# Inverse stage 1 in blocks of 512 columns, joint evictions of the rest columns, and late F2 in 64-column tiles

## The chip, the cores and the metric

One core of a Trainium2 chip runs the whole program. The metric is the device time of one execution in microseconds; the number given for a kernel is the median of its runs.

## The reference

Two branches work on the same layer-normed input and are joined at the end. `S` is 2048, `D` is 640, `F` is 1728.

```python
xn = _layernorm(q)
# branch A: short shift filter, gate, long convolution by FFT over 2S points, gate
kv = sum(k_pad[:, t:t + S, :] * shift_k[:, ks - 1 - t] for t in range(4)) * v
y  = irfft(rfft(pad(kv)) * rfft(pad(ssm_k)))[:, :S] + kv * ssm_D
s  = xn * y
# branch B: MLP
g  = silu(gelu_tanh(xn @ w1 + b1) @ w2 + b2)
out = q + s * g
```

## The kernel before

The convolution is done as matrix products with tables of sines. The points lie on 128 partitions by 16 tiles of 640 columns. **Stage 1** (`K1`, `K1r` for the filter, `U1`, `U1r` for kv, lines 321 and 332) multiplies each tile by the table `W`; the first 512 columns of a tile are one PSUM tile, and the last 128 columns ("rest") of two tiles share another. They are evicted (`Ke`, `Ker`, `Ue`, `Uer`) into one of four `st` buffers, and each of eight blocks is written to the scratch tensors `scrK` and `scrU` (`Ks`, `Us`) and read back in another layout (`KL`, `UL`). **Stage 2** (`K2`, `U2`, line 500, and `X2` for the rest columns of both, line 515) multiplies by the small table `F2_t` and is evicted in place (`Kf`, `Uf`). Then DVE forms products (`pr`, line 532) into `st` buffers, **inverse stage 1** (`i1`, line 542) multiplies them by the small table `I1_t`, the result is evicted (`ie`) and goes through `scrC` (`cs` writes, `cl` reads); **inverse stage 2** (`i2`, line 568) multiplies by `G`, the transpose of `W`, and DVE multiplies the result into xn (`ym`), adds x (`ad`) and SP stores it (`os`). The kv products are 5 groups on DVE (`kv0` to `kv4`).

The MLP works on four chunks of four tiles. F1 (`f1`, line 402, and `f1h` for the last 64 rows, line 416) gives 14 row blocks of the hidden layer, each followed by a gelu on ACT (`ge`, `geh`); F2 (`f2_i_h`, line 437) does tile i in two column halves of 320, 14 matmuls each, followed by a silu (`si`, line 441) and a product (`gx`, line 443). Transposes of xn (`xt`, line 382) and their evictions (`xe`) come before F1.

PSUM has two small buffers for the MLP (`psf`) and three of two banks for the convolution (`ps`). `evict` (line 166) is a copy on ACT or on DVE, as the order says.

The order of all operations is one list written out by hand, `ORDER`; `Plan.emit` walks through it, takes the first free slot of each pool and emits the operation on its engine (a suffix `/A` or `/D` says ACT or DVE for evictions). Each engine runs its part in that order and waits where an operand or a buffer isn't ready. DMAs are issued from SP's queue, in the same order; a write waits there for its evictions, and what stands behind it waits too.

```python
for n, token in enumerate(tokens):
    ...
    for b in o.bufs:
        ...
        k = next(s for s in slots if all(left[a] == 0 for a in b.pool.after[s]))
    o.fn(e)
```

`warm` (line 594) runs matmuls on zeros at the start. `sm0` (POOL) and `sm1` (DVE) compute the angles for the two small tables, `ss` (ACT, lines 263 and 264) takes their sines.

Of the kernel before, what the change touches and what calls it, by code (L numbers as in the profile page):

```python
# [33 lines left out]
XTD = ()  # L34

# [62 lines left out]
def h3_block(ctx: ExitStack, tc: tile.TileContext, x_d, k_d, v_d, sk_d, K_d, D_d, w1_d, b1_d, w2_d, out_d):  # L98
# [29 lines left out]
    sl_t = [sb.tile([P, H], BF16, name="sl%d" % i)[:] for i in range(3)]  # L128
# [33 lines left out]
    def dmaq(e):  # L162
        return (nc.gpsimd if e == "POOL" else nc.sync).dma_start
# [43 lines left out]
    for g in range(2):  # L207
        a, b = TB[g], TB[g + 1]

        def wq(e, a=a, b=b):  # L210
            n = b - a
            nc.vector.tensor_tensor(out=Pm[:, a:b, :], in0=tq[:, a:b, None].to_broadcast([P, n, 64]),
                                    in1=mq[:, None, :].to_broadcast([P, n, 64]), op=ALU.mult)
            nc.vector.tensor_single_scalar(out=Pc[:, a:b, :], in_=Pm[:, a:b, :], scalar=3 * L // 4, op=ALU.add)
            nc.vector.tensor_single_scalar(out=Pc[:, a:b, :], in_=Pc[:, a:b, :], scalar=L - 1, op=ALU.bitwise_and)
            nc.vector.tensor_single_scalar(out=Pm[:, a:b, :], in_=Pm[:, a:b, :], scalar=L - 1, op=ALU.bitwise_and)
# [18 lines left out]
    def sm1(e):  # L235
# [5 lines left out]
        bit(bi[0], pi, 31, ALU.bitwise_and)  # L241
        bit(bi[1], bi[0], 1, ALU.arith_shift_right)
        bit(bi[2], bi[0], 1, ALU.bitwise_and)
        bit(bi[3], pi, 5, ALU.arith_shift_right)
        bit(bi[3], bi[3], 1, ALU.bitwise_and)
        g.tensor_copy(out=k2s, in_=bi[0])
        g.tensor_copy(out=n2s, in_=bi[1])
        g.tensor_scalar(out=c1s, in0=bi[2], scalar1=16.0, scalar2=None, op0=ALU.mult)
        g.tensor_tensor(out=n2s, in0=n2s, in1=c1s, op=ALU.add)
        g.tensor_scalar(out=c0s, in0=bi[3], scalar1=-8.0, scalar2=24.0, op0=ALU.mult, op1=ALU.add)  # L250
        g.tensor_scalar(out=c1s, in0=bi[3], scalar1=24.0, scalar2=None, op0=ALU.mult)
        for w, c in enumerate((c0s, c1s)):
# [103 lines left out]
    hT, xnT, sl = Pool(hT_t, after=[[], [zb, tmb, smb]]), Pool(xnT_t), Pool(sl_t)  # L356
# [37 lines left out]
    for c in range(NCH):  # L394
        for r, (a, b) in enumerate(((0, 256), (256, 512)) if c == 0 else ((0, 512),)):
            for ft in range(FT - 1):
                pb = Buf(pool=psf)
                nm = "%d_%d_%d" % (c, r, ft)

                def f1(e, c=c, ft=ft, a=a, b=b, pb=pb):  # L400
                    for t in range(DT):
                        nc.tensor.matmul(out=pb.v[:, 0:b - a], lhsT=w1_t[:, ft, t, :], rhs=xnTb[c].v[:, a // P:b // P, t, :],  # L402
                                         start=(t == 0), stop=(t == DT - 1))

                def ge(e, c=c, ft=ft, a=a, b=b, pb=pb):
                    nc.scalar.activation(out=hTb[c].v[:, ft, a:b], in_=pb.v[:, 0:b - a], func=ACT.Gelu_apprx_tanh,  # L406
                                         bias=b1_f[:, ft:ft + 1], scale=1.0)
# [20 lines left out]
    def f2_tile(i):  # L428
        c, q = divmod(i, CH)
        for h in range(2):  # L430
            pb, s_ = Buf(pool=psf), Buf(pool=sl)
            hs = slice(h * H, (h + 1) * H)

            def f2(e, pb=pb, hs=hs):
                for ft in range(FT):
                    M = P if ft < FT - 1 else FLAST + 1
                    nc.tensor.matmul(out=pb.v[:, 0:H], lhsT=hTb[c].v[0:M, ft, q * P:(q + 1) * P], rhs=w2_t[0:M, ft, hs],  # L437
                                     start=(ft == 0), stop=(ft == FT - 1))

            op("f2_%d_%d" % (i, h), "PE", f2, reads=[hTb[c]] + hTf[c] + w2b + oneb, writes=[pb], hold=[s_])  # L440
            op("si_%d_%d" % (i, h), "ACT", lambda e, pb=pb, s_=s_: nc.scalar.activation(  # L441
                out=s_.v, in_=pb.v[:, 0:H], func=ACT.Silu), reads=[pb], writes=[s_])
            op("gx_%d_%d" % (i, h), "DVE", lambda e, s_=s_, hs=hs: nc.vector.tensor_tensor(  # L443
                out=xn_t[:, i, hs], in0=xn_t[:, i, hs], in1=s_.v, op=ALU.mult), reads=[s_], writes=[xnb[i][h]])
# [39 lines left out]
    Kall = []  # L484
    for s in range(NG):
# [33 lines left out]
        for w, (nm, B) in enumerate((("K", Ks), ("U", Us))):  # L519
            op("%sf_%d_2" % (nm, s), "ACT|DVE", lambda e, B=B, pb=pb, w=w: evict(  # L520
                e, B.v[:, :, 512:D].rearrange("p (a r) c -> p a r c", r=2),
                pb.v.rearrange("p a (r w c) -> p a r w c", r=2, w=2)[:, :, :, w, :]), reads=[pb], writes=[sp[nm][2]], hold=[B])
        for hh in range(2):
            hs = slice(hh * H, (hh + 1) * H)
            pr = Buf(pool=st)
            prb = [Buf(), Buf()]
            for w in range(2):
                def prod(e, w=w, hs=hs, Ks=Ks, Us=Us, pr=pr):
                    o = pr.v.rearrange("p a d -> p (a d)").rearrange("p (w a r c) -> p w a r c", w=2, a=2, r=2)[:, w]
                    u = Us.v[:, :, hs].rearrange("p (a r) c -> p a r c", r=2)  # L530
                    k = Ks.v[:, :, hs].rearrange("p (a r) c -> p a r c", r=2)[:, :, w:w + 1, :].to_broadcast([P, 2, 2, H])
                    nc.vector.tensor_tensor(out=o, in0=u, in1=k, op=ALU.mult)  # L532
# [155 lines left out]
```

## Time and profile before

| | |
|---|---|
| median of 3 runs | 193.66 us (193.22 to 194.75) |
| profiled execution | 193.75 us, of which the span is 192.0 us |
| PE busy | 179.7 us, 94% of the span |
| DVE busy | 161.6 us, 84% |
| ACT busy | 139.1 us, 72% |
| DMA | 51.13 MB, 266 GB/s over the span |
| granted PE clock | 0.972 in the mean |

The span goes from the first to the last instruction; the profiled time is 1.75 us longer. An engine's busy time is the time in which at least one of its instructions ran; matmuls overlap, so a busy PE can still have gaps between the starts of its matmuls. A row of a timeline or of the chain begins with its start and its length in us; "x14" is the number of instructions in it. In a row by stages each engine has its busy time and, in brackets, its number of instructions; then come the granted PE clock, the DMA engines' busy share and GB/s.

### The profile page before, as it was taken

What the parts mean: (1) busy time and instruction counts of PE and PEld (TensorE: products, weight loads), DVE (VectorE), ACT (ScalarE), POOL (GpSimd) and SP (SyncE); (2) the same over time, 40 slices, a digit from 0 to 9 for tenths busy, and PEclk for the clock granted to TensorE, in tenths of its full rate; (3) what the DMA queues carried; (4) which work ended last, traced back from release to release, by engine and by line L of the source; (5) the groups of instructions that cost most, each with busy time, mean ns of one, the idle gap of its engine ahead of it and who ended that gap; (6) DMA issues with size and microseconds to landing.
All of it is one profiled execution on the core that took longest, in us unless ns stands there. A gap on an engine that the chain in (4) does not pass through costs nothing.

```text
span 192.0 us, 4825 instructions
## 1 busy us (share of the span) xinstructions
PE 179.7 (94%) x1993; PEld 99.8 (52%) x1993; DVE 161.6 (84%) x273; ACT 139.1 (72%) x220; POOL 14.0 (7%) x28
## 2 busy tenths in 40 slices
PE   7289999999999999999999998999989999999991
PEld 2045776544356666655644344334344567666570
DVE  7996999999999999998779976899986631299993
ACT  4394879999899979996889797997988761201110
POOL 8321200005200000002000000000000000000000
PEclk9756999999999999999999999999999999999999
DMA  6998779996969999999799498529405434989573
GB/s 150 369 383 333 307 207 399 353 368 192 386 261 312 337 377 304 342 417 329 241 364 360 142 235 238 165 48 371 165 3 202 160 130 116 412 262 340 198 262 116
DMA packets 24423, 51.13 MB, mean 266 GB/s; under 512 B 3665, under 2 KB 18386, under 8 KB 24018
## 3 DMA queue, kind: packets, MB, share of 16 engines
q1 hardware_dynamic: 24256, 50.83, 76.5%
q8 instruction: 15, 0.25, 0.5%
q14 instruction: 6, 0.05, 0.1%
q10 hardware_dynamic: 146, 0.00, 0.0%
HBM read 31.95 MB, written 18.35 MB: 262 GB/s over the span
## 4 chain that ended last, share of the span: by engine, by line
PE 67%; DVE 18%; ACT 11%; issue 2%; POOL 0%; DVEq 0%; POOLq 0%
PE psf L402 27%; PE psf L437 24%; DVE xn L572 5%; PE ps L542 5%; PE ps L500 4%; PE ps L321 4%; ACT st L166 3%; DVE x L576 2%; ACT hT L406 2%; ACT ku L166 2%; ACT hT L422 2%; PE psf L382 2%; DVE ku L166 1%; DVE xn L443 1%; PE ps L515 1%
## 5 line engine op out<-in xcount | busy, mean ns | idle before, releaser
L402 PE MATMUL psf<-xnT,w 128*128 128x512 bf16 (+1 forms) x325 | 65.8, 346 | 1.3 <-DVE b1f L291 0.7
L437 PE MATMUL psf<-w,hT 128*128 128x320 bf16 x448 | 64.8, 299 | 0.0
L437 PEld LDWEIGHTS <-hT 128*128 128x128 bf16 x448 | 42.3, 98 | 19.8 <-issue 3.9
L402 PEld LDWEIGHTS <-w 128*128 128x128 bf16 x325 | 30.0, 100 | 32.4 <-issue 13.7
L406 ACT ACTIVATE hT<-psf,b1f 128x512 bf16<-128x512 f32 (+1 forms) x65 | 39.0, 614 | 7.0 <-PE psf L402 5.7
L166 ACT CAST ku<-ps 128x640 bf16<-128x640 f32 (+2 forms) x48 | 37.0, 805 | 6.1 <-DVE ku L166 2.9
L166 ACT CAST st<-ps 128x1024 bf16<-128x1024 f32 (+1 forms) x45 | 38.0, 907 | 0.1
L441 ACT ACTIVATE sl<-psf 128x320 bf16<-128x320 f32 x32 | 14.7, 459 | 29.4 <-PE psf L437 26.8
L166 DVE CAST ku<-ps 128x1024 bf16<-128x1024 f32 (+2 forms) x32 | 29.9, 952 | 6.5 <-PE ps L542 2.2
L532 DVE TENSOR_TENSOR st<-ku 128x1280 bf16<-128x1280 bf16 x32 | 24.6, 817 | 1.7 <-PE ps L542 1.3
L443 DVE TENSOR_TENSOR xn<-xn,sl 128x320 bf16<-128x320 bf16 x32 | 10.1, 318 | 15.1 <-ACT sl L441 14.4
L470 DVE TENSOR_TENSOR ku<-ku 128x2560 bf16<-128x2560 bf16 (+1 forms) x15 | 18.3, 1217 | 0.3
L467 DVE TENSOR_TENSOR ku<-ku 128x2560 bf16<-128x2560 bf16 (+1 forms) x15 | 18.2, 1216 | 0.0
L542 PE MATMUL ps<-st,I 32*64 32x320 bf16 x512 | 13.1, 300 | 1.7 <-ACT ku L166 1.7
L353 DVE BATCH_NORM_STATS2 stats<-x 128x6 f32<-128x320 bf16 x32 | 13.7, 468 | 0.0
L572 DVE TENSOR_TENSOR xn<-ps,xn 128x640 bf16<-128x640 f32 x16 | 12.5, 813 | 0.0
L542 PEld LDWEIGHTS <-I 32*64 32x64 bf16 x512 | 7.3, 103 | 8.7 <-issue 7.4
L500 PE MATMUL ps<-ku,F 64*32 64x512 bf16 x256 | 10.0, 380 | 0.0
L166 ACT COPY xnT<-psf 128x640 bf16<-128x640 bf16 x11 | 8.0, 725 | 0.7 <-PE psf L382 0.7
L382 PE MATMUL psf<-ident,xn 128*128 128x128 bf16 x80 | 7.5, 231 | 0.4 <-ACT hT L406 0.3
L366 POOL TENSOR_SCALAR rstd<-mv 128x4 f32<-128x4 f32 (+1 forms) x5 | 2.3, 454 | 70.6 <-DVE mv L354 68.9
L382 PEld LDWEIGHTS <-xn 128*128 128x128 bf16 x80 | 5.5, 103 | 3.2 <-issue 1.9
(67 smaller groups left out, 119.9 us busy)
## 6 DMA issues: line engine op xcount, KB each, us to landing
scrK<-st SPq DMA_DIRECT2D x8, 640.0 KB, 4.2
scrU<-st SPq DMA_DIRECT2D x8, 640.0 KB, 4.9
ku<-scrK SPq DMA_DIRECT2D x8, 640.0 KB, 5.4
ku<-scrU SPq DMA_DIRECT2D x8, 640.0 KB, 8.2
scrC<-ku SPq DMA_DIRECT2D x8, 640.0 KB, 4.5
ku<-scrC SPq DMA_DIRECT2D x8, 640.0 KB, 6.4
ku<-in_v SPq DMA_DIRECT2D x4, 640.0 KB, 6.5
out<-x SPq DMA_DIRECT2D x15, 160.0 KB, 1.9
```

The costliest lines, as they stand in the source:

```text
L166: (nc.scalar.copy if e == "ACT" else nc.vector.tensor_copy)(out=out_, in_=in_)
L382: nc.tensor.transpose(out=o[:, t, :], in_=xn_t[:, i, t * P:(t + 1) * P], identity=ident[:])
L402: nc.tensor.matmul(out=pb.v[:, 0:b - a], lhsT=w1_t[:, ft, t, :], rhs=xnTb[c].v[:, a // P:b // P, t, :], start=(t == 0), stop=(t == DT - 1))
L406: nc.scalar.activation(out=hTb[c].v[:, ft, a:b], in_=pb.v[:, 0:b - a], func=ACT.Gelu_apprx_tanh, bias=b1_f[:, ft:ft + 1], scale=1.0)
L437: nc.tensor.matmul(out=pb.v[:, 0:H], lhsT=hTb[c].v[0:M, ft, q * P:(q + 1) * P], rhs=w2_t[0:M, ft, hs], start=(ft == 0), stop=(ft == FT - 1))
L441: op("si_%d_%d" % (i, h), "ACT", lambda e, pb=pb, s_=s_: nc.scalar.activation(out=s_.v, in_=pb.v[:, 0:H], func=ACT.Silu), reads=[pb], writ ...
L467: op("kv%d_%dm" % (r, j), "DVE", lambda e, i=i, n=n, j=j, t=t, wb=wb: nc.vector.tensor_tensor(out=t.v[:, 0:n, :], in0=k_t[:, i + 3 - j:i + ...
L470: op("kv%d_%da" % (r, j), "DVE", lambda e, n=n, t=t, a=a: nc.vector.tensor_tensor(out=a.v[:, 0:n, :], in0=a.v[:, 0:n, :], in1=t.v[:, 0:n, ...
L500: nc.tensor.matmul(out=pb[ri].v[32 * j:32 * j + 32, a, :], lhsT=F2_t[64 * a:64 * a + 64, ri, :], rhs=B.v[64 * a:64 * a + 64, j, 0:512], st ...
L532: nc.vector.tensor_tensor(out=o, in0=u, in1=k, op=ALU.mult)
L542: nc.tensor.matmul(out=pb[j // 2].v[64 * a:64 * a + 64, j % 2, 0:H], lhsT=I1_t[32 * j:32 * j + 32, m, :], rhs=o[32 * j:32 * j + 32, w, a, ...
L572: op("ym_%d" % i, "DVE", lambda e, i=i, pb=pb: nc.vector.tensor_tensor(out=xn_t[:, i, :], in0=pb.v.rearrange("p a b -> p (a b)")[:, 0:D], ...
```

## The change

- Inverse stage 1. A block's first 512 columns are done in one piece: two products (`pm`) of 2048 elements into two `st` buffers, 32 matmuls of 512 columns (`j1`), two evictions (`je`) of 1024. The rest columns are multiplied per block (`pq`, two of 512 elements), but two blocks share one `st` buffer, 32 matmuls of 256 columns (`j1r`) and two evictions (`jer`) of 512. The `scrC` writes of two blocks stand together behind `jer`.
- The rest columns of stage 2 of filter and kv are evicted by one instruction (`Xf`, 1024 elements) where there were two of 512.
- F2 of tiles 8 to 15: each matmul of 128 output rows becomes two of 64, which write partitions 0 to 63 and 64 to 127 of the same PSUM tile.
- The last tile is split in 416 and 224 columns where it was 320 and 320, and its wide part comes first.
- F1 of chunk 0: pairs of row blocks share a PSUM tile (2 x 256 columns), and row block 12 is done over 512 columns.
- The small tables' angles use fewer instructions, live in `G_t`, and `sm1` and `ss` stand later in the order. `wq` is split in two.
- 25 warming matmuls where there were 12.
- A new `ORDER`.

```diff
+        def stage3(pb, rhs, n):
+            for m, (w, r, t) in enumerate(((0, 0, 0), (0, 1, 1), (1, 0, 1), (1, 1, 2))):
+                for j in range(4):
+                    for a in range(2):
+                        nc.tensor.matmul(out=pb[j // 2].v[64 * a:64 * a + 64, j % 2, 0:n], lhsT=I1_t[32 * j:32 * j + 32, t, :],
+                                         rhs=rhs(slice(32 * j, 32 * j + 32), w, 2 * a + r), start=(m == 0), stop=(m == 3))
...
+        pm = [Buf(pool=st) for _ in range(2)]
...
+        if x == 0:
+            pq, pqb, Ur, Cr = Buf(pool=st), [], [], []
...
-                    nc.tensor.matmul(out=pb.v[:, 0:H], lhsT=hTb[c].v[0:M, ft, q * P:(q + 1) * P], rhs=w2_t[0:M, ft, hs],
-                                     start=(ft == 0), stop=(ft == FT - 1))
+                    for m, n in ((0, 64), (64, P)) if i >= F2C else ((0, P),):
+                        nc.tensor.matmul(out=pb.v[m:n, 0:hw], lhsT=hTb[c].v[0:M, ft, q * P + m:q * P + n], rhs=w2_t[0:M, ft, hs],
+                                         start=(ft == 0), stop=(ft == FT - 1))
...
-NWARM = 12
+NWARM = 25
 ORDER = """
...
+grid xl1 id zz c0 warm fix xl0 one0 sm0 wq1 wr1 xl3 bn1 bn0 rs0 Dl b1l Kl1 ws1 Kl3 K1_6 Ke_6/A bn5 bn7 b1c xl2 K1r_2
+xn0 w1l1 xn1 Ker_2/A bn6 one1 bn4 K1r_3 xt0 Ker_3/A xe0/A K1_4 wq0 wr0 K1r_7 Ke_4/A K1_7 rs2 Ke_7/A Ker_7/A ws0 K1_5
+xt1 xe1/D bn2 bn3 w1l3 xn5 xn4 f1_0_0_2 xn6 K1_12 ge_0_0_2 ge_0_0_3 xn7 rs1 f1_0_0_10 K1_13 ge_0_0_11 ge_0_0_10 wxl
...
+Uer_1/A ge_0_1_9 f1_0_1_0 Us_0 ge_0_1_0 ge_0_1_1 K1r_4 K1_8 Ke_9/A f1_0_1_6 ge_0_1_7 ge_0_1_6 f1_1_0_10 f2_2_1
+ge_1_0_10 f2_0_1 bn12 ss sx si_2_1 gx_2_1 bn13 Ker_4/A bn15 Ke_8/A f2_2_0 kl3 bn14 si_0_1 vl2 U1r_2 Uer_2/A si_2_0
...
+Us_5 KL3 Us_6 U1_15 bn8 gx_3_0 bn9 bn10 Ue_15/A U1_14 xt13 xe13/A f2_4_0 si_4_0 bn11 K2_2 Ue_14/A Kf_2_0/D Kf_2_1/A
+xt14 Us_7 xe14/D f2_0_0 gx_4_0 rs3 xn9 K2_1 si_0_0 Kf_1_1/A f2_6_0 xn8 Kf_1_0/A xt9 K2_3 si_6_0 KL0 gx_7_1 xn11 xe9/D
+xt8 xn10 gx_6_0 Kf_3_0/D xe8/A gx_0_0 f2_7_0 si_7_0 Kf_3_1/A xt11 K2_0 f2_1_0 gx_7_0 UL0 X2_0 Kf_0_1/D Kf_0_0/A U2_0
...
+cs_2 cs_3 pm_7_1 j1_6 ge_2_0_9 f2_10_0 je_6_0/A cs_5 je_6_1/D cs_4 si_10_0 cs_6 j1_7 f2_9_0 je_7_1/A je_7_0/D gx_10_0
+si_9_0 f2_11_1 f2_11_0 cs_7 cl_5 cl_3 si_11_1 si_11_0 gx_9_0 f2_10_1 si_10_1 gx_11_0 gx_10_1 f2_9_1 si_9_1 f2_8_1
+i2_11 i2_10 f1h_3 si_8_1 i2_7 gx_9_1 gx_11_1 ym_11 ym_10 ym_7 i2_6 f2_8_0 geh_3 si_8_0 cl_1 cl_6 cl_4 i2_3 i2_2 ym_6
...
+f2_15_0 si_15_0 os_14 f2_15_1 si_15_1 ym_15 gx_15_0 ad_15_0 os_15_0 gx_15_1 ad_15_1 os_15_1
```

More of the change, by code (lines that the diff above doesn't have):

```diff
@@ L34 @@
 XTD = ()
+F2C = 8
+LAST = 416
 class Buf:
@@ L484, in h3_block, with slots @@
     Kall = []
+    def slots(K, U):
+        k0 = [m for m in range(4) if kl.views[m] is K.v][0] * 4
+        u0 = [m for m in range(7) if ul.views[m] is U.v][0] * 4 + NT + 3
+        return k0, u0
     for s in range(NG):
@@ L553, in h3_block @@
+                op("jer_%d_%d" % (s // 2, u), "ACT|DVE", jer, reads=[pb[u]] + pqb, writes=[cw], hold=Ur)
+            for y in (s - 1, s):
+                op("cs_%d" % y, "SP", lambda e, y=y, Us=Ur[y % 2]: dmaq(e)(out=by_t(scrC)[y], in_=Us.v), reads=Cr[y % 2] + [Ur[y % 2]], writes=[sCb[y]])
     for i in range(8, FLIP):
```

234 lines of the change are left out of this document (116 added, 118 removed).

## The prediction, made before the changed kernel was run

> **What bounds the kernel now.** I read the page's engine shares first, then stages, then the chain that ended last. The stages below are cut where the first late matmul of each part starts; the columns are busy times of the engines.
>
> ```profile
> PE 179.7 (94%) x1993; PEld 99.8 (52%) x1993; DVE 161.6 (84%) x273; ACT 139.1 (72%) x220; POOL 14.0 (7%) x28
> ...
> 0.00:8.98 8.98, 4.10 (x12) 1.52 (x13) 7.67 (x28) 3.43 (x3) 5.89 (x19) 0.91 0.80 253
> 8.98:30.30 21.32, 20.07 (x150) 13.54 (x150) 19.11 (x40) 15.85 (x32) 2.94 (x5) 0.80 0.86 311
> 30.30:54.83 24.53, 24.19 (x167) 11.92 (x166) 24.20 (x33) 23.36 (x38) 3.88 (x2) 1.00 0.91 345
> 54.83:96.63 41.80, 41.80 (x401) 26.18 (x407) 38.24 (x61) 37.37 (x56) 1.25 (x2) 1.00 0.91 321
> 96.63:154.81 58.18, 56.38 (x991) 25.19 (x999) 48.54 (x62) 51.69 (x77) 0.00 (x0) 1.00 0.65 203
> 166.95:187.70 20.75, 20.75 (x177) 13.00 (x176) 19.92 (x41) 3.50 (x8) 0.00 (x0) 1.00 0.78 269
> ```
>
> PE runs without a gap from 54.8 to 96.6 and from 154.8 to 187.7. In the first 30 us it starts late and on a lowered clock (0.80); in 30.3:54.8 ACT is the full one (23.36 of 24.53); in 96.6:154.8 PE, DVE and ACT take turns. So I count PE's own work in written order and call the rest lost time. The paces come from the chain:
>
> ```profile
> 97.19 1.19 PE psf L402 x5
> ...
> 99.42 2.27 PE psf L402 x10
> ...
> 152.79 2.01 PE psf L437 x14
> 155.48 11.55 PE psf L437 x84
> ```
>
> A half tile of F2 (14 matmuls of 320 columns) takes 2.01 when other shapes stand around it, and 11.55/6 = 1.925 in a run of six. Ten F1 matmuls of 512 columns take 2.27, five take 1.19. So a change of array shape costs about 0.10 (2.01 - 1.91, and 2 x 1.19 - 2.27), and a matmul costs 0.136 at 320 columns and 0.217 at 512: 0.42 ns a column and 2.5 ns fixed. By that pace the old order is 154.2 us of streaming and 118 changes of shape at 0.097, together 165.6 us of PE work. Against the times of the trace PE has lost 16.8 us where the first F2 starts (54.7; 37.9 of work stand before it), 17.3 at the first U2 (96.6; 79.3), 21.8 at the last i1 (154.7; 132.9) and 22.1 at the end.
>
> **The change, part by part.** The sum is made against the profiled execution: 192.0 of span and 1.75 around it, 193.75; the median is 193.66, the same within 0.05%. A measurement of this kernel tells about 1% from no change.
>
> T1, PE work. F2's late tiles become pairs of 64-column matmuls that write the two halves of the PSUM tile. No F2 of that form is in the trace, but F1's half tile has the same 128 x 64 shape:
>
> ```profile
> L437 PEld LDWEIGHTS <-hT 128*128 128x128 bf16 x416 | 39.1, 98 | 18.6 <-issue 3.9
> L416 PEld LDWEIGHTS <-w 128*64 128x64 bf16 x40 | 1.9, 109 | 0.7 <-issue 0.5
> ...
> 114.99 0.74 PE L416 MATMUL psf<-xnT,w 128*64 128x256 bf16 x10
> 115.66 0.41 PE L515 MATMUL ps<-ku,F 64*32 64x256 bf16 x16
> ```
>
> Forty loads of 109 ns would be 4.4 us one by one, and the row has 1.9 busy, so the two column halves load side by side. Ten matmuls hold PE from 114.99 to 115.66, 0.67; without the change of shape that is 0.114 a pair of 256 columns, the pace of one full-width matmul. So the pair of 320 costs 0.136 as before, and the bounds are 0.136 and 0.272. What is gained is that F2 and i2 now have one shape:
>
> ```profile
> 170.84 2.08 PE L437 MATMUL psf<-w,hT 128*128 128x320 bf16 x14
> 172.84 1.01 PE L568 MATMUL ps<-ku,G 128*64 128x512 bf16 x12
> ```
>
> 170.84 to 172.84 is 2.00 for 1.905 of streaming; those changes go. Inverse stage 1 turns sixteen blocks of 32 matmuls of 320 columns into eight of 512 and four of 256 columns: the same columns, four blocks fewer. The new order has 102 changes of shape and 154.1 us of streaming, 164.0. **T1 = -1.6.**
>
> T2, start. Thirteen more warming matmuls run before the first data and cost nothing there:
>
> ```profile
> 3.28 0.15 PEld L594 LDWEIGHTS <-hT 128*128 128x128 bf16 x1 [0.28 <-issue]
> 3.70 0.15 PEld L594 LDWEIGHTS <-hT 128*128 128x128 bf16 x1 [0.28 <-issue]
> 4.03 0.75 PEld L594 LDWEIGHTS <-hT 128*128 128x128 bf16 x4 [0.17 <-issue]
> ...
> 8.98 0.13 PEld L332 LDWEIGHTS <-W 64*128 64x128 bf16 x3 [2.55 <-issue]
> ```
>
> They go at 0.43 (3.28, 3.70) until about 3.9 and then near 0.21, so 25 end at about 7.9, before the 8.98 of the first filter block; if the clock stayed halved they would end at 11.9 and cost 2.9. I take 0. The filter's load still has 0.98 MB ahead of it on SP's queue (a piece of w1 and two x tiles give their place to four other x tiles). The small tables' DVE chain (16 instructions, from 6.6 to 9.4) leaves the start, and ACT's two small sines too (0.63); x's statistics move in. What bounds this stretch is then ACT: in the new order it has 41.7 us of work from the first filter eviction to the first F2 (15 Ke and 4 Ue at 0.90, 9 of the rest columns at 0.48, 24 gelus at 0.37, 13 at 0.58, and others, each from its start to the next one's in runs), and 1.28 for the gelu table. It starts at 9.4, so F2 cannot start before 52.4. ACT's idle time from 8.98 to 54.83 was 45.9 - 15.85 - 23.36 = 6.6 in the old; 5.5 of it in the first 21 us, where ACT had little but narrow gelus to do. The new order gives it K evictions there, but two pairs of gelus still wait for a slow F1, and the transposes for PSUM. I take 3.0: F2 at 55.4 with 40.2 of PE work before it, so 15.2 lost instead of 16.8. **T2 = -1.6**, between -4.6 (no idle) and +2.0 (6.6 as now).
>
> T3, the two small sines now stand between the last gelu and the first silu. Two loads of ACT's function table where there was one:
>
> ```profile
> 12.64 1.28 ACT L406 ACT_TABLE_LOAD   x1
> 13.94 0.47 ACT L406 ACTIVATE hT<-psf,b1f 128x256 bf16<-128x256 f32 x1
> ...
> 56.16 0.71 ACT L406 ACTIVATE hT<-psf,b1f 128x512 bf16<-128x512 f32 x1
> 56.89 1.28 ACT L441 ACT_TABLE_LOAD   x1
> 58.19 0.44 ACT L441 ACTIVATE sl<-psf 128x320 bf16<-128x320 f32 x1
> ```
>
> From the end of the last F1: gelu to +0.75, table 1.28, sines 0.63, table 1.28, first silu 0.33, so +4.3. PE covers 3.84 of it with two half tiles, because psf has two buffers and the third waits for that silu. Queued behind the sines are that silu, Ker_4 and Ke_8, and PE's next F2 and U1r_2 behind those. **T3 = +0.3 to 0.5; I take 0.3.** A second such place, geh_3 between two silus in the last stage, costs two more loads; ACT is busy 3.50 of 20.75 there, and f2_8_0 (1.9) covers the gelu that f2_13_1 needs. I cost it at nothing; without the cover it is 1.3.
> [...]
>
> T4, scrU's round trip. The last block's eviction Ue_14 now stands behind a silu that waits for a whole half tile of F2. In PE's work the write Us_7 can go out at 69.7 and X2_0, which needs the first U block back, stands at 79.5: 9.8 us. The old needed
>
> ```profile
> 80.00 5.67 SPq L339 DMA_DIRECT2D scrU<-st  x4
> 85.77 0.46 SPq L488 DMA_DIRECT2D ku<-scrK  x1
> 91.25 6.41 SPq L489 DMA_DIRECT2D ku<-scrU  x7
> ...
> ku<-scrU SPq DMA_DIRECT2D x1, 640.0 KB, 4.3
> ```
>
> from the last write (85.4) to 91.25, and 4.3 for the first block back: 10.2. On SP's queue KL0 stands between them and seven loads behind the wait. **T4 = +0.5** (0 to 2).
>
> T5, the middle, from U2_0 to j1_7. PE's work falls from 53.6 to 49.8, since f2_10_1 and F1's last half tile move behind j1_7. DVE's does not fall:
>
> ```profile
> L532 DVE TENSOR_TENSOR st<-ku 128x1280 bf16<-128x1280 bf16 x32 | 24.6, 817 | 1.7 <-PE ps L542 1.3
> L467 DVE TENSOR_TENSOR ku<-ku 128x2560 bf16<-128x2560 bf16 x9 | 13.3, 1481 | 0.0
> L166 DVE CAST ku<-ps 128x512 bf16<-128x512 f32 x10 | 6.7, 684 | 1.0 <-PE ps L515 1.0
> L166 ACT CAST ku<-ps 128x640 bf16<-128x640 f32 x24 | 16.0, 703 | 1.4 <-PE ps L542 1.2
> L166 ACT CAST ku<-ps 128x1024 bf16<-128x1024 f32 x18 | 18.0, 1014 | 1.6 <-PE ps L500 1.3
> ```
>
> By 817 at 1280 elements and 1481 at 2560 (0.52 ns an element), a product of 2048 takes 1.22 and one of 512 takes 0.42: two of each are 3.27, as four of 817. The 512 is in runs of 128 with gaps; were it as slow as the eviction of that size (0.684), 16 of them would add 4.3. I take the lower, as 817 is already for runs of 320. Evictions shift: eight joint Xf of 1024 stand for sixteen of 512, sixteen je and eight jer for 32 of 640, so ACT falls by some 3.6 and DVE gains 1.1. DVE then has 49.3 in this stretch, PE 49.8. Two engines with equal work that wait for each other through four st buffers cannot both run full. DVE was busy 48.54 of 58.18, but in its better windows more:
>
> ```profile
> sum 30.00, PE 29.59 PEld 11.91 DVE 28.36 ACT 26.96 POOL 0.00; mean PE 9.86 PEld 3.97 DVE 9.45 ACT 8.99 POOL 0.00
> ```
>
> (100:110, 120:130, 130:140: 94%.) I take 91%: 49.3 / 0.91 = 54.2, so PE loses 4.4 where it lost 4.5. **T5 = -0.2.** Bounds: PE's pace with a little loss (51.3, -3.1) and DVE idle as now (59.8, +5.4).
>
> T6, the end. From j1_7 to the first i2 PE has six half tiles, as before (11.55). The round trip took
>
> ```profile
> 156.42 0.36 SPq L551 DMA_DIRECT2D scrC<-ku  x1
> 160.87 2.07 SPq L560 DMA_DIRECT2D ku<-scrC  x4
> ```
>
> 4.5 to the reads, and the first block had landed by 166.95, so the six still cover it. Behind it PE has 22.0 and DVE 21.0, in the old 20.6 and 20.3 without a loss; cost 0, and DVE's lead of 1.0 is the cover. After the last F2 the chain was
>
> ```profile
> 188.03 0.33 DVE L443 TENSOR_TENSOR xn<-xn,sl 128x320 bf16<-128x320 bf16 x1 [0.46 <-DVE xn L572]
> ...
> 188.99 0.33 DVE L584 TENSOR_TENSOR x<-xn,x 128x320 bf16<-128x320 bf16 x1
> ```
>
> It becomes silu, product and sum of 224 columns instead of 320 (0.05 less for each on DVE, 0.08 on ACT), with the other half's pair done before. **T6 = -0.3.**
>
> Sum: -1.6 - 1.6 + 0.3 + 0.5 - 0.2 - 0.3 = -2.9; 193.75 - 2.9 = **190.9**.
>
> **Rivals.**
> A, no gain at the start: ACT idles 6.6 as now, T2 = +2.0, 194.5. For it: the first gelus still wait on PE at a low clock. Against: ACT's first work no longer waits for the small tables.
> B, the middle at PE's pace: T5 = -3.1, 188.0. For it: PE has 26 F1 pieces that need no product, and three of its losses there were single waits of about 1 us. Against: DVE at 96%.
> C, slower: st's four buffers. A j1 needs two whole product tiles and the pair's rest columns hold a third, so of the next group only one tile can be written until j1 is through; DVE stands in order behind the other, with evictions that PE waits for. A wait is a piece of F1 and the j1 itself, 1.19 + 0.87 = 2.05, less what DVE can do first (a rest product and a small eviction, about 1.2): 0.8 for seven groups, 5.6, so 196.5. It decides once DVE's idle time in the middle passes 7.8 (4.9 + 2.9). For it: L532 waited for PE once (1.3) even with half-sized products. Against: only once.
> D, column halves that load one after the other: 2 x 109 = 218 a pair instead of 136, 224 pairs, +18.4, 209. Against it is L416's 1.9 busy. [...]
> [...]
>
> **How the numbers follow.** Forecast 0.41, own range 189.3 to 192.5 (T2 and T5 each moved by about 1.5); B 0.17, A 0.14, C 0.23, D 0.03, E 0.02. The 1% bounds are 191.7 and 195.6. Faster: 0.33 of the forecast, all of B, 0.02 of A: 0.52. Same: 0.08, A's 0.10, E's 0.02 and 0.02 of C: 0.22. Slower: 0.26. The range goes from 187.0 (B, with T2 a little better) to 196.5 (C); outside are D, half of C's upper side and the far end of B.
>
> **What would show it.** T1: F2 rows of 128x64 starting in pairs, and no gap ahead of i2. T2: first F2 near 55.4, ACT over 93% busy from 9 to 55. T3: a table load, two sines, a table load in a row, and less than 0.5 of PE idle. T4: U2_0 near 95.9. T5: j1_7 54 after it; DVE over 90% between. T6: PE without a gap behind. The prediction is wrong if the first F2 starts after 58, if L532's successors wait more than 5 us for PE, or if the late F2 takes more than 2.0 a half tile.

## The result, and the profile after

The changed kernel takes 188.62 us in the median (four runs, 186.23 to 189.31) where the kernel before takes 193.92. The ratio is 0.9696, 95% interval 0.9609 to 0.9783: faster. Ratios leave out runs that lie more than 1.5% above the fastest of their kernel, so a ratio isn't always the quotient of the medians. The forecast was 190.9, its range 187.0 to 196.5.

The profiled execution was the fastest of them, 186.23 with a span of 184.5, and it shows a granted clock of 1.00 where the others have 0.98. I therefore ran the unchanged text of the changed kernel once more (after_again: 188.94, span 187.2, clock 0.981), and use that profile wherever a typical run is meant.

The engines' shares and the stages of the changed kernel, in the profiled execution. The columns of the stages are as in the prediction: length, busy time of PE, PEld, DVE, ACT and POOL, granted clock, DMA share, GB/s.

```profile
PE 175.7 (95%) x2097; PEld 103.9 (56%) x2097; DVE 160.5 (87%) x262; ACT 139.0 (75%) x210; POOL 14.1 (8%) x29
```

```profile
8.93:30.11 21.18, 18.30 (x150) 10.48 (x150) 19.95 (x48) 20.10 (x31) 2.52 (x4) 1.00 0.93 331
30.11:54.41 24.30, 24.06 (x183) 13.82 (x180) 22.19 (x17) 23.96 (x44) 0.00 (x0) 1.00 0.95 353
54.41:95.17 40.76, 40.21 (x389) 25.52 (x395) 36.90 (x73) 32.64 (x50) 5.92 (x5) 1.00 0.91 324
95.17:146.18 51.01, 51.01 (x845) 21.20 (x823) 49.60 (x56) 46.91 (x63) 0.00 (x0) 1.00 0.66 209
146.18:158.65 12.47, 12.47 (x204) 9.94 (x204) 3.09 (x8) 4.04 (x8) 0.00 (x0) 1.00 0.67 235
158.65:180.80 22.15, 22.15 (x330) 20.02 (x324) 20.81 (x44) 7.53 (x13) 0.00 (x0) 1.00 0.78 279
```

The middle (95.17 to 146.18) stands out: 51.0 us where the old one took 58.2, PE without a gap, and DVE busy 49.60 of 51.01, 97%, where it was 83%. Of the 7.2 us, 3.8 is PE work that the new order puts behind this stage (53.6 and 49.8 by the count); the rest is time that PE no longer loses. The two stages behind it have no PE gap either.

The same stages up to the first F2 in the second profile, and the stretch in it in which the clock was halved:

```profile
8.93:30.11 21.18, 18.50 (x130) 9.81 (x131) 17.62 (x48) 17.43 (x27) 2.52 (x4) 0.84 0.81 291
30.11:57.18 27.07, 26.83 (x204) 15.56 (x204) 25.86 (x18) 26.73 (x48) 0.00 (x0) 1.00 0.95 353
...
12.87:19.69 6.82, 6.00 (x29) 3.35 (x28) 4.52 (x14) 4.60 (x8) 2.28 (x3) 0.50 0.91 332
```

Here the first F2 starts at 57.18, 2.8 later than in the first profile. PE was at half speed for 6.82 us, and ACT, which gets its work from PE, was busy only 17.43 of the 21.18 where it was 20.10.

Counted as in the prediction (start of an instruction less the PE work that stands before it in written order), the lost time is, in us:

| lost until | before | after, profiled | after_again |
|---|---|---|---|
| first F2 | 16.8 | 14.2 | 17.0 |
| U2_0 | 17.3 | 15.4 | 18.2 |
| last stage 3 of the middle (i1_7_0; j1_7) | 21.8 | 16.6 | 19.3 |
| last matmul | 22.1 | 16.7 | 19.5 |
| PE work in all | 165.6 | 164.0 | 164.0 |
| from there to the end of the span | 4.3 | 3.8 | 3.8 |

So a typical execution gains 1.6 on PE's work, 3.3 in the middle (1.2 lost instead of 4.5), 0.2 in the late stage and 0.4 at the end. It gives back 0.2 at the start and 0.6 between the first F2 and U2_0. That is 4.7, as the spans say (192.0 and 187.2). Where the clock isn't halved it gains 2.7 more.

What the old kernel lost in the middle can largely be seen in its PE timeline. Most of its sixteen i1 blocks of 32 matmuls run through. Three stop after four matmuls, where the second of their two PSUM buffers comes in, and wait for an eviction on ACT:

```profile
107.70 0.75 PE L542 MATMUL ps<-st,I 32*64 32x320 bf16 x32
108.38 1.25 PE L402 MATMUL psf<-xnT,w 128*128 128x512 bf16 x5
110.00 0.33 PE L542 MATMUL ps<-st,I 32*64 32x320 bf16 x4 [0.37 <-ACT ku L166]
110.60 0.73 PE L542 MATMUL ps<-st,I 32*64 32x320 bf16 x28 [0.27 <-ACT ku L166]
111.26 1.25 PE L402 MATMUL psf<-xnT,w 128*128 128x512 bf16 x5
...
117.70 0.33 PE L542 MATMUL ps<-st,I 32*64 32x320 bf16 x4
118.47 0.73 PE L542 MATMUL ps<-st,I 32*64 32x320 bf16 x28 [0.45 <-ACT ku L166]
119.31 1.24 PE L402 MATMUL psf<-xnT,w 128*128 128x512 bf16 x5
...
142.68 0.33 PE L542 MATMUL ps<-st,I 32*64 32x320 bf16 x4
143.59 0.74 PE L542 MATMUL ps<-st,I 32*64 32x320 bf16 x28 [0.57 <-ACT ku L166]
144.25 1.25 PE L402 MATMUL psf<-xnT,w 128*128 128x512 bf16 x5
```

A block that runs through takes 0.68 to the next start (107.70 to 108.38). These three take 1.26, 1.61 and 1.57, 2.4 more together, and 0.37 of idle time stands ahead of the first: 2.8 of the 4.5 lost. In the changed kernel PE has no idle time in the middle, so its 1.2 there is no wait; it lies spread thinly over all blocks.

The rows of the changed operations, each shape apart (busy, mean ns, idle before):

```profile
L439 PEld LDWEIGHTS <-hT 128*64 128x64 bf16 x416 | 24.9, 110 | 4.0 <-issue 0.8
L537 DVE TENSOR_TENSOR st<-ku 128x2048 bf16<-128x2048 bf16 x16 | 19.1, 1217 | 0.2
L537 DVE TENSOR_TENSOR st<-ku 128x512 bf16<-128x512 bf16 x16 | 6.0, 416 | 0.0
```

The products cost what was worked out for them (1.22 and 0.42), and the loads of 64 columns stand beside matmuls: 28 of them go with a half tile that holds PE for 1.90, as this late part of PE's timeline shows.

```profile
158.65 0.71 PE L610 MATMUL ps<-ku,G 128*64 128x512 bf16 x8
159.19 0.71 PE L417 MATMUL psf<-xnT,w 128*64 128x256 bf16 x10
159.73 0.73 PE L610 MATMUL ps<-ku,G 128*64 128x512 bf16 x8
160.28 2.09 PE L439 MATMUL psf<-w,hT 128*64 128x320 bf16 x28
162.18 0.73 PE L610 MATMUL ps<-ku,G 128*64 128x512 bf16 x8
```

From 160.28 to 162.18 is 1.90 (14 x 0.136), and the next i2 starts without the gap of about 0.1.

### The profile page after: what moved, and what is told of

Same layout as the page of the kernel before. It is cut to its first block, busy times and chain, and to the rows that moved or that the text cites. A ratio compares the mean times of both kernels' runs of the same rounds, so it can differ in the third digit from the quotient of the medians.

```text
span 184.5 us, 5000 instructions
## 1 busy us (share of the span) xinstructions
PE 175.7 (95%) x2097; PEld 103.9 (56%) x2097; DVE 160.5 (87%) x262; ACT 139.0 (75%) x210; POOL 14.1 (8%) x29
## 4 chain that ended last, share of the span: by engine, by line
PE 81%; ACT 11%; DMA 4%; issue 1%; DVE 1%; SPq 1%; ACTq 0%
PE psf L439 31%; PE psf L403 29%; PE ps L543 6%; ACT st L170 5%; PE ps L508 5%; DMA x<-in_ssm_k 4%; PE ps L322 3%; PE ps L610 2%; PE psf L383 2%; ACT hT L409 2%; PE ps L522 1%; PE ps L333 1%; ACT hT L423 1%; ACT sl L443 1%; ACT L443 1%
## 5 line engine op out<-in xcount | busy, mean ns | idle before, releaser
L439 PE MATMUL psf<-w,hT 128*64 128x320 bf16 (+6 forms) x672 | 64.9, 299 | 0.6 <-ACT sl L443 0.5
L439 PEld LDWEIGHTS <-hT 128*64 128x64 bf16 (+3 forms) x672 | 48.1, 106 | 15.3 <-issue 4.1
L170 ACT CAST ku<-ps 128x1024 bf16<-128x1024 f32 (+1 forms) x37 | 34.0, 952 | 3.2 <-PE ps L543 1.3
L443 ACT ACTIVATE sl<-psf 128x320 bf16<-128x320 f32 (+2 forms) x32 | 14.1, 442 | 29.0 <-PE psf L439 28.1
L170 DVE CAST ku<-ps 128x1024 bf16<-128x1024 f32 (+1 forms) x27 | 31.5, 1179 | 2.0 <-PE ps L543 1.0
L537 DVE TENSOR_TENSOR st<-ku 128x512 bf16<-128x512 bf16 (+1 forms) x32 | 24.8, 816 | 0.2
L445 DVE TENSOR_TENSOR xn<-xn,sl 128x320 bf16<-128x320 bf16 (+2 forms) x32 | 9.9, 315 | 11.0 <-ACT sl L443 11.0
L472 DVE TENSOR_TENSOR ku<-ku 128x2560 bf16<-128x2560 bf16 (+1 forms) x15 | 18.3, 1221 | 0.3
L469 DVE TENSOR_TENSOR ku<-ku 128x2560 bf16<-128x2560 bf16 (+1 forms) x15 | 18.3, 1220 | 0.2
L614 DVE TENSOR_TENSOR xn<-ps,xn 128x640 bf16<-128x640 f32 x16 | 12.6, 815 | 1.2 <-PE ps L610 1.2
L543 PE MATMUL ps<-st,I 32*64 32x512 bf16 (+1 forms) x384 | 11.2, 344 | 0.0
L636 PE MATMUL psf<-hT 128*128 128x512 bf16 x25 | 7.4, 467 | 1.2 <-DVE cst L194 1.2
L474 DVE TENSOR_TENSOR ku<-ku 128x2560 bf16<-128x2560 bf16 (+1 forms) x5 | 6.1, 1222 | 1.8 <-DMA ku<-in_v 1.7
```

Source lines behind the costliest of these rows:

```text
L170: (nc.scalar.copy if e == "ACT" else nc.vector.tensor_copy)(out=out_, in_=in_)
L439: nc.tensor.matmul(out=pb.v[m:n, 0:hw], lhsT=hTb[c].v[0:M, ft, q * P + m:q * P + n], rhs=w2_t[0:M, ft, hs], start=(ft == 0), stop=(ft == F ...
L443: op("si_%d_%d" % (i, h), "ACT", lambda e, pb=pb, s_=s_, hw=hw: nc.scalar.activation(out=s_.v[:, 0:hw], in_=pb.v[:, 0:hw], func=ACT.Silu), ...
L469: op("kv%d_%dm" % (r, j), "DVE", lambda e, i=i, n=n, j=j, t=t, wb=wb: nc.vector.tensor_tensor(out=t.v[:, 0:n, :], in0=k_t[:, i + 3 - j:i + ...
L472: op("kv%d_%da" % (r, j), "DVE", lambda e, n=n, t=t, a=a: nc.vector.tensor_tensor(out=a.v[:, 0:n, :], in0=a.v[:, 0:n, :], in1=t.v[:, 0:n, ...
L543: nc.tensor.matmul(out=pb[j // 2].v[64 * a:64 * a + 64, j % 2, 0:n], lhsT=I1_t[32 * j:32 * j + 32, t, :], rhs=rhs(slice(32 * j, 32 * j + 3 ...
```

## The experiments

Each is the changed kernel with one edit, unless it says otherwise. Lost times are counted as above, the middle from U2_0 to the last stage 3. Between executions with a different granted clock I compare only what comes after the start.

**The change of array shape: F2 in full-width matmuls again.**

```diff
-F2C = 8
+F2C = NT
```

> The changed kernel with F2 of tiles 8 to 15 in full-width matmuls again; order and all else as changed. By my count the changes of array shape go from 102 back to 118. Theory S (late F2 gains only by the shape it shares with i2, 0.097 us a change): +1.5 us against the changed kernel, all of it after j1_7, where F2 and i2 alternate. Rival (column halves gain nothing, or their two weight loads cost something): 0 or less than 0. Rival (late stage bound by DVE's products, so PE's changes of shape are hidden): under 0.5.

190.34 us, ratio to before 0.9823 (0.9772 to 0.9874). The timeline has the old gaps back:

```profile
164.09 0.73 PE L610 MATMUL ps<-ku,G 128*64 128x512 bf16 x8
164.75 2.08 PE L439 MATMUL psf<-w,hT 128*128 128x320 bf16 x14
166.76 0.73 PE L610 MATMUL ps<-ku,G 128*64 128x512 bf16 x8
```

From 164.75 to 166.76 is 2.01 for what took 1.90 above. From j1_7 to the last F2 half this kernel takes 34.97 (147.76 to 182.73) and after_again 33.16: 1.81 for 16 changes of shape, of which 16 x 0.097 = 1.55 was expected. The 64-column tiles are worth at least what they were costed at.

**The start: 12 warming matmuls again.**

```diff
-NWARM = 25
+NWARM = 12
```

> The changed kernel with 12 warming matmuls, as before the change, instead of 25. Theory W (the longer warming keeps the granted clock at full speed past the first data, and the first F1 pieces need it): the clock halves from about 7 to 17 us as in the kernel before, F1 at 14 us runs at half pace, ACT waits for its first gelus: +1 to +2 us. Rival (that stretch is bound by ACT's evictions, so PE's clock does not matter): within 0.5 us.

188.26, ratio 0.972 (0.9665 to 0.9775): no loss against 188.94. The clock was lowered in this profile too (0.979 in the mean, 0.981 in after_again), but from 10.50 on and not from 12.87. Its clock line, in slices of 4.64 us:

```profile
PEclk9966999999999999999999999999999999999998
```

The first F2 came at 55.53 instead of 57.18, so the price of a lowered clock isn't fixed. The thirteen more matmuls neither help nor hurt the time.

**The start: matmuls on zeros between the first K blocks.**

```diff
+    def fill(e, n):
+        for _ in range(n):
+            nc.tensor.matmul(out=psf_t[1], lhsT=hT_t[1][:, 0, 0:P], rhs=hT_t[1][:, 0, :], start=True, stop=True)
+FILL = (2, 1, 1, 2, 6)
```

The five groups stand behind K1r_3, xt0, K1_4, K1r_7 and K1_7.

> The changed kernel with 12 more zero matmuls of 512 columns put in PE's gaps between 9.3 and 13.2 us (2, 1, 1, 2 and 6 of them behind K1r_3, xt0, K1_4, K1r_7 and K1_7), so that PE is not idle before the first F1. The four unprofiled runs of the changed kernel had a clock of 0.98 and spans of 186.8 to 187.5, the profiled one 1.00 and 184.5. Theory W (the difference is the halved clock at the start, let in by PE's idle time between 8 and 14 us): every run at 1.00 and near 184.5 of span, so about -2 us in the median against the changed kernel. Rival (the halving comes whatever PE does there, or PE's clock at the start does not matter): within 0.5 us, or slower by the up to 1 us that the zero matmuls stand in the way.

187.13, all four runs between 186.91 and 187.46, ratio 0.9659 (0.962 to 0.9699). No run had a halved clock (0.999 to 1.000). The clock line of the two profiles, in tenths over 40 slices, after_again first:

```profile
PEclk9985899999999999999999999999999999999999
```

```profile
PEclk9999999999999999999999999999999999999999
```

The matmuls on zeros kept the clock up: the four runs of after_again, on the same chip without them, have 0.979 to 0.988. The 6.00 busy of 6.82 above is no measure of PE's work, as matmuls take longer at half speed: fifteen F1 matmuls of 256 columns hold PE for 3.31 us in the kernel before (14.01 to 17.32, clock 0.50), 0.22 each, and ten hold it for 1.20 in the first profile of the changed kernel (15.77 to 16.97, clock 1.00), 0.12 each. The 3.42 us ahead of the halving, between the last matmul of the warming (9.13) and the first F1, are sparse (after_again):

```profile
9.45:12.87 3.42, 1.81 (x23) 0.89 (x19) 3.30 (x12) 3.32 (x5) 0.24 (x1) 1.00 1.03 427
```

In the kernel before, the clock was at 0.50 for 10.24 us, and PE was busy 1.36 of the 3.42 us ahead of that:

```profile
3.91:7.33 3.42, 1.36 (x6) 0.48 (x5) 3.28 (x16) 2.15 (x2) 1.54 (x4) 1.00 1.00 359
7.33:17.57 10.24, 7.90 (x46) 4.36 (x45) 9.86 (x32) 6.05 (x12) 2.74 (x5) 0.50 0.96 361
```

PE's busy time alone doesn't tell the two executions of the changed kernel apart. In the first profile, whose clock stayed at 1.00, the same 3.42 us are no fuller:

```profile
9.45:12.87 3.42, 1.62 (x17) 0.78 (x14) 3.31 (x12) 3.42 (x6) 0.37 (x2) 1.00 1.02 415
```

Why the clock falls in one execution and not in another isn't shown by these runs.

The fill isn't free: the first F1 starts at 14.98 instead of 14.27, and one late matmul waits for a transfer:

```profile
PE ps L610 <- DMA ku<-scrC: 0.4, 1, 0.4
```

**The changed kernel once more.**

> The changed kernel once more, as a measure for the other three on the same chip: 0.97 of the kernel before. If the clock at the start differs from one execution to the next, its runs fall into two groups, near 186.3 and near 188.7.

188.94, ratio 0.9746 (0.9684 to 0.9808). The lost time at f1h_1 was 13.1 at a mean clock of 1.00 (after), 14.7 at 0.991 (u1_f2_full) and 15.9 at 0.981 (after_again), but 14.3 at 0.979 in u2_warm12, whose clock fell earlier. The kernel before, at 0.972, started its first F2 at 54.7 all the same. So the changed start is limited by ACT when the clock is full (ACT busy 97% from 8.93 to the first F2 in after), and by PE's pace when it isn't (ACT 92% in after_again).

**The small tables early again.**

```diff
-... bn1 bn0 rs0 Dl b1l Kl1 ws1 Kl3 ...    ... sm1 kv0_0 ...    ... bn12 ss sx si_2_1 ...
+... bn1 bn0 sm1 rs0 Dl b1l Kl1 ws1 ss sx Kl3 ...    ... kv0_0 ...    ... bn12 si_2_1 ...
```

> The changed kernel with the small tables at the start again: sm1 on DVE behind the first statistics, the sines ss behind the large ones on ACT, the scaling sx next. It takes two table loads and 0.63 us of sines off the place between the last gelu and the first silu (PE lost 0.7 there) and puts 9 small DVE instructions and the sines ahead of the first xn and the first filter evictions. Theory T (tables late are a net gain because the start is bound by ACT's and DVE's first work): slower by 0.5 to 1.5 us. Rival (ACT has idle time before the first filter block at 8.9, so early tables cost nothing there and save the 0.7): -0.5 to -0.8 us.

187.61, ratio 0.9717 (0.968 to 0.9753). In the changed kernel ACT's timeline at the first silu is the row of loads that the prediction described:

```profile
53.80 1.31 ACT L409 ACTIVATE hT<-psf,b1f 128x256 bf16<-128x256 f32 x2
55.13 1.28 ACT L264 ACT_TABLE_LOAD   x1
56.42 0.35 ACT L264 ACTIVATE F<-G,cst 128x64 bf16<-128x64 int32 x1
56.68 0.44 ACT L265 ACTIVATE I<-G,cst 128x192 bf16<-128x192 int32 x1
57.13 1.28 ACT L443 ACT_TABLE_LOAD   x1
58.43 0.44 ACT L443 ACTIVATE sl<-psf 128x320 bf16<-128x320 f32 x1
```

and PE waits behind it for the third half tile:

```profile
54.41 3.97 PE L439 MATMUL psf<-w,hT 128*128 128x320 bf16 x28
58.92 1.38 PE L439 MATMUL psf<-w,hT 128*128 128x320 bf16 x9 [0.54 <-ACT sl L443]
```

The lost time rises from 14.24 to 14.94 over these two half tiles, 0.7. With the tables early it rises by 0.01 (15.96 to 15.97), and the first F2 starts only 0.14 later than in u1_f2_full, whose clock was lowered too (56.13 and 55.99). The mean clocks are 0.987 here and 0.991 there; the 0.92 from 8.93 to 30.11 here means some 3.4 us at half speed, an estimate from that share. Some 0.3 of the 0.7 came back here as other losses before U2_0. So the late tables lose about 0.4 there and win some 0.1 at the start, a net loss of about 0.3; the expectation's rival (0.5 to 0.8) was nearer than its theory.

**The middle: joint evictions split in two.** `Xf` and `je` become two instructions each, everything else stays.

```diff
+            for w, V in enumerate((K, U)):
+                evict(e, V.v[:, :, 512:D].rearrange("p (a r) c -> p a r c", r=2),
+                      pb.v.rearrange("p a (r w c) -> p a r w c", r=2, w=2)[:, :, :, w, :])
...
-                e, Us.v[:, 2 * u:2 * u + 2, 0:512], pb[u].v), ...
+                e, Us.v[:, 2 * u:2 * u + 2, c:c + 256], pb[u].v[:, :, c:c + 256]) for c in (0, 256)], ...
```

> The changed kernel and order, but each joint eviction of rest columns (Xf) is two of 512 elements again, and each je two of 512: 24 more instructions on ACT and DVE in the middle, some 0.06 us each on ACT and 0.08 on DVE, 1.7 us in all, and twice the instructions that PE's PSUM buffers wait for. Theory O (the middle lost only 1.2 us instead of my 4.4 because of where the new order puts products and evictions, not because they are fewer): at most +1 us. Rival F (fewer, larger instructions are what made the middle run through): +2.5 us or more, toward the 4.4 lost of the forecast.

187.81 (186.08 to 189.74; before on the same chip 193.11). The middle loses 1.5 where it loses 1.2 unsplit (profiled span 184.7 against 184.5), far from the 4.5 of before. The size of these evictions isn't what speeds the middle up.

**The middle: rest products done twice**, 16 more products on DVE.

```diff
-... lambda e, ...: prod(e, pqv()[:, w, :, x, :]..., slice(512, D), w),
+... lambda e, ...: [prod(e, pqv()[:, w, :, x, :]..., slice(512, D), w) for _ in range(2)],
```

> The changed kernel with every rest product (pq) done twice: 16 more DVE instructions of about 0.34 us in the middle, 5.4 us. DVE was busy 42.23 of 43.20 us between 103.0 and 146.2, PE 43.20. Theory B2 (both engines are full in the middle, DVE has 1 us to spare there): +3 to +5 us. Rival (PE alone is the bound and DVE could still be ahead of it): under +1.5 us.

195.06, ratio 1.0098 (1.0062 to 1.0133). The middle and PE's waits in it:

```profile
96.96:154.64 57.68, 52.26 (x845) 22.04 (x826) 56.08 (x72) 47.60 (x63) 0.00 (x0) 1.00 0.58 185
```

```profile
PE ps L508 <- DVE ku L170: 3.0, 4, 1.3
PE ps L543 <- DVE ku L170: 2.2, 2, 1.9
```

DVE is again at 97% (56.08 of 57.68). It has 6.5 us more work (56.08 and 49.60), not the 5.4 of the expectation, as a rest product takes 0.416. The middle is 6.7 longer: all of the added work, and a little more, is on the path, and the time is about 6 above that of the changed kernel on another chip (188.94), more than the 3 to 5 expected. DVE has next to no slack in the changed kernel.

**The middle: less PE work.** F1 of chunks 2 and 3 sums over four of its five parts of D, which leaves out one matmul of 512 columns in each of 26 pieces in the middle.

```diff
+                    dt = DT - 1 if c >= 2 else DT
```

> The changed kernel with one of the five contraction tiles left out in F1 of chunks 2 and 3 (24 pieces, 24 matmuls of 512 columns fewer, 5.2 us of PE work in the middle). Theory B2 (both engines full): PE's gain is taken by DVE at once, -1 to -2 us only. Rival (PE alone is the bound): -5 us.

187.34, ratio 0.9614 (0.9537 to 0.9692).

```profile
97.01:146.78 49.77, 48.20 (x819) 20.18 (x798) 48.79 (x56) 46.45 (x63) 0.00 (x0) 1.00 0.68 214
```

The middle has 26 PE instructions fewer (819 and 845), which is 5.6 us at 0.217; the expectation counted 24. That shortens the middle by 1.2 (51.0 to 49.8), with DVE at 98%. Together with the run before: both engines are full, and relieving PE alone gives little. What relieving DVE alone would give wasn't tried.

**The middle: the same instructions in a poorer order.** 29 of the 32 products move behind the next eviction on DVE, never past their reader.

```diff
-... U2_1 pq_0_0 pq_0_1 X2_1 ... Uf_1_1/D pm_1_1 ... ge_2_0_11 pm_0_1 pq_1_0 pq_1_1 je_1_0/D pm_0_0 ...
+... U2_1 X2_1 ... Uf_1_1/D pq_0_0 pq_0_1 pm_1_1 ... ge_2_0_11 je_1_0/D pm_0_1 pq_1_0 pq_1_1 ... Uf_2_0/D pm_0_0 ...
```

> The changed kernel with 29 of the 32 products of the middle moved, each behind the next eviction that stands after it on VectorE (never past the stage 3 that reads it); same instructions, same engines. Theory O (the middle runs full because of where its products and evictions stand): the loss between U2_0 and j1_7, 1.2 us in the changed kernel, grows to 3 to 7, waits of PE for st and of VectorE for PE appear, and the time is 190.5 to 195. Rival B2 (VectorE and PE have equal work there and the buffers are enough for any sensible order): the loss stays under 2.2 and the time within 188 to 190.

194.98, ratio 1.0073 (1.0042 to 1.0105): 0.7% slower than the kernel before. The middle, and what PE waits for in it:

```profile
97.52:155.28 57.76, 51.57 (x845) 21.74 (x824) 49.26 (x56) 47.27 (x63) 0.00 (x0) 1.00 0.57 185
```

```profile
PE ps L543 <- DVE st L537: 3.9, 3, 1.6
PE ps L543 <- DVE ku L170: 1.9, 2, 1.7
PE ps L508 <- DVE ku L170: 0.4, 1, 0.4
```

DVE has the same work (49.26), but is busy 85% of 57.76 instead of 97%. The middle loses 7.9 instead of 1.2, more than the 3 to 7 expected of the theory. PE waits 3.9 for products and 2.3 for evictions; the changed order has none of these waits. With the same instructions, the order alone decides whether the two engines run full.

**The kernel before, with only f1h_3 and geh_3 moved out of its middle.**

```diff
-... ie_5_0_0/A f1h_3 i1_5_1 Kf_6_2/D pr_6_0_1 Uf_6_2/A geh_3 f1_2_0_2 ...   ... i2_0 i2_1 i2_13 ... f2_12_1 i2_12 ...
+... ie_5_0_0/A i1_5_1 Kf_6_2/D pr_6_0_1 Uf_6_2/A f1_2_0_2 ...   ... i2_0 i2_1 f1h_3 i2_13 ... f2_12_1 geh_3 i2_12 ...
```

> The kernel before with only f1h_3 and geh_3 moved from the middle to behind the first two i2, as the change does. Theory W (the middle's losses of the kernel before are single waits of PE for an eviction that stands behind gelus on ACT): the loss from U2_0 to the last i1, 4.5, falls by 0.8 to 1.8, and 0.6 of PE work moves behind it, so the time falls by 0.8 to 1.8 from that of the kernel before. Rival (another wait takes the place at once): the loss falls by less than 0.5 and the time is within 0.6 of the kernel before; two more table loads late (1.28 each) cost nothing, or up to 1.3 if a silu there is waited for.

193.18, ratio 0.9971 (0.9945 to 0.9998). The middle loses 4.3 instead of 4.5, and PE's waits take another form:

```profile
PE ps L542 <- ACT ku L166: 1.1, 3, 0.4
PE ps L542 <- DVE ku L166: 0.6, 1, 0.6
```

where the kernel before had this one row for its middle:

```profile
PE ps L542 <- ACT ku L166: 1.7, 4, 0.6
```

The i1 block that waited at 142.68 behind the two gelus of geh_3 runs through here, and the block ahead of it now waits 0.58 for an eviction on DVE. One wait went and another came; this move alone doesn't give the 3.3.

**Tables early, and a lighter fill.** The edits of u4_tables_early and n1_warm_fill together, with nine matmuls on zeros instead of twelve.

```diff
-FILL = (2, 1, 1, 2, 6)
+FILL = (2, 1, 1, 0, 5)
```

> The changed kernel with the small tables' vector and sine work back at the start (as in u4_tables_early) and with nine matmuls on zeros between the first K blocks (2 after K1r_3, 1 after xt0, 1 after K1_4, 5 after K1_7; n1_warm_fill had twelve). Theory: the clock is full in every execution (1.3 us for each 3.4 us window it is halved in otherwise), the 0.7 at the first silu is gone, so 186.0 to 187.0 with all runs within 0.6. Rival: the matmuls on zeros push the first F1 back as in n1_warm_fill (14.98 instead of 14.27) and the tables push back the first gelus, which gives both gains back: 187.1 to 188.2. If nine are too few, windows of halved clock come back and single runs lie at 188 and above.

186.54, four runs between 186.51 and 186.57, ratio 0.9628 (0.9591 to 0.9665): the best version. The clock is full (0.998 to 1.000), the first two half tiles of F2 lose 0.01, and the late wait for a transfer is gone. The first F1 still starts at 15.22, 0.9 later than in the profiled execution of the changed kernel, which costs what the early tables gain: the spans are the same (184.5). What the version adds is that every execution is as good as that one.

**The same with f1h_3 back in the middle.**

```diff
-... Xf_6/D f1_3_0_10 j1_4 ge_3_0_10 je_4_0/A ...   ... i2_10 f1h_3 si_8_1 ... f2_8_0 geh_3 si_8_0 ...
+... Xf_6/D f1_3_0_10 f1h_3 j1_4 ge_3_0_10 geh_3 je_4_0/A ...   ... i2_10 si_8_1 ... f2_8_0 si_8_0 ...
```

> n2_tables_fill with the half tile f1h_3 and its gelu geh_3 back in the middle (behind f1_3_0_10, ahead of j1_4) instead of the last stage. Theory (the last stage is PE's alone, the middle is VectorE's): 0.67 us of PE work and two loads of ACT's table leave a stage in which PE never waits, and the middle takes them for 0.2 (a change of array shape) to 0.5: 0.2 to 0.5 faster than n2_tables_fill. Rival (both engines are full in the middle, as d1_pq_twice and p1_less_f1 showed): the middle's loss grows by 0.5 to 1.0 as the stage 3 behind comes later and two gelus stand ahead of an eviction on ACT; no gain, or 0.4 slower.

187.18 (187.16 to 187.20), ratio 0.966 (0.9616 to 0.9705), 0.64 slower than n2_tables_fill. Neither account was quite right. The middle lost no more (1.2 in both) but grew by the 0.65 of PE work that came in. The late stage, freed of that work, didn't get shorter: its length from i2_11 to the last F2 half is 20.7 in both, and it has a new wait:

```profile
PE ps L610 <- DVE xn L614: 0.4, 1, 0.4
```

L614 is `ym`, the product of inverse stage 2 on DVE. That stage is full on DVE too (20.81 of 22.15), so the PE work that the change put there was free.

## Why the prediction was right, and where its steps weren't

The time, 188.62, lies in the range and on the predicted side, 2.3 below the forecast. It lies outside the forecast's own range (189.3 to 192.5) and next to rival B (188.0), and it was B's middle that came, to which the prediction gave 0.17. That the number fits is partly luck, as two errors met: the middle came out 3.1 better than forecast and the start 1.8 worse. The execution with the full clock took 186.23, below the whole range.

**T1** (-1.6) held. PE's work is 164.0, the late F2 has the pace of a full-width one, the loads of 110 ns lie beside the matmuls (rival D falls), and putting the shape changes back cost 1.8.

**T2** (-1.6) didn't come in a typical execution: +0.2. With the clock at 1.00 throughout it was -2.6 (16.8 to 14.2). The step that failed is the allowance of 3.0 of ACT idle time, which took PE's pace in the first 20 us as given. In after_again ACT is idle 21.18 - 17.43 = 3.75 up to 30.1 alone, in the profiled execution 1.08. From 8.93 to the first F2 it was busy 92% in the one and 97% in the other. The prediction named the lowered clock only as an argument for rival A and as a price of the warming; it should have been a term of its own. The 25 warming matmuls ended at 8.56 and 9.13 in the two profiles, not at 7.9, and still cost nothing by u2_warm12.

**T3** (+0.3) measured 0.7, of which the wait itself is the 0.54 above, just over the 0.5 named as its sign; the shape of the stall, two half tiles of cover and PE waiting for that silu, was as described. The loads took 1.28, and the next activation started 1.29 and 1.30 after a load did (55.13 to 56.42, 57.13 to 58.43). No run shows a load that holds ACT for twice its row, which is the E that has 0.02 among the chances. The second such place, geh_3, cost nothing, as assumed.

**T4** (+0.5) was 0: in the stage from 54.41 to 95.17 PE's idle time is 0.55, and 0.54 of it is that silu.

**T5** (-0.2) was the term that was mis-sized: the middle lost 1.2, not 4.4, so T5 was -3.3, just past the low bound of -3.1. The count of work was right (PE 49.8 by the count, DVE 49.3 expected and 49.60 measured). What failed is the choice of 91% for DVE, argued from "two engines with equal work that wait for each other through four st buffers cannot both run full". They can: in the changed kernel PE has no gap and DVE is at 97%. The old loss of 4.5, which the prediction took as the measure, was for 2.8 the wait of three i1 blocks for an eviction on ACT; rival B had these waits in view. Rival C's mechanism, DVE held up for lack of a free `st` buffer, didn't come. Nor does the poorer order show it: its 194.98 is near C's 196.5, but no wait of DVE for an `st` buffer stands among DVE's waits there (the largest is 2.6, of evictions for PE's inverse stage 1), and PE waits for products and evictions that come late.

What took the old waits away isn't put down to one part of the change. Split evictions and one moved half tile change the middle's loss by 0.3 at most, so neither of the two does it. The column split wasn't undone by itself: with halves of 320 a rest product would need the evictions of the main columns too, and several stand behind it in the new order, so it couldn't be tried without another order. How much of the freedom to order so well comes from the column split stays open.

**T6** (-0.3) was -0.4 at the end, with PE without a gap behind j1_7, as expected.

The errors partly cancelled: T2 and T3 came out 1.8 + 0.4 worse, T4 and T5 0.5 + 3.1 better, T6 0.1 better; the late stage gained another 0.2 that no term had.

## What to carry over

Where two engines have nearly equal work in a stage, the order of their instructions can decide how full they run, here between 97% and 85% of DVE, or 6.7 us of 51. A share read from a stage that was ordered otherwise says little about the one to come: look first at which waits make it up (here three blocks), and give both ends of the range a real chance. Count PE's work in written order and look at the lost time at each landmark: a term of the sum can then be checked by itself. Before a gain at the start is booked, see whether the granted clock there is the same in every execution (here 0.98 and 1.00 for one kernel), whether PE has gaps there (matmuls on zeros in them went with a clock of 0.998 or above here), and give the clock a term of its own.

## What the runs showed of the hardware that was not expected

The changed kernel had its clock at 1.00 throughout one execution (after) and at 0.50 from 12.87 to 19.69 in another (after_again); the kernel before had it at 0.50 from 7.33 to 17.57. PE was busy 1.81 and 1.36 of the 3.42 us ahead of these two stretches, and 1.62 of the 3.42 us from 9.45 in the execution without one. With the same start the first F2 came at 54.3 and 54.4 in profiles with a mean clock of 1.00 (s1_split, after), at 56.0 to 56.2 with 0.987 to 0.991 (u1_f2_full, d1_pq_twice, p1_less_f1) and at 56.7 and 57.2 with 0.981 (o1_pm_later, after_again). Nine or twelve matmuls on zeros among the sparse ones kept the clock at 0.998 or above in all runs of three kernels; with nine, the four times of a kernel lie within 0.06 us.

PE and DVE were busy 100% and 97% of 51 us while they fed each other through four `st` buffers.
